# One chunk-causal attention and two MLPs on one core: a planner with other rules for results, ports and slots, and two score banks as one tile

## The chip, the cores and the metric

The kernel runs on one core of a Trainium2 chip. The metric is the device time of one execution in microseconds (us): the median of three runs of the kernel before is 953.37 us (953.12 to 954.3). Engines are named as the profile names them: PE (TensorE), DVE (VectorE), ACT (ScalarE), POOL (GpSimd), SP (SyncE, which issues the DMAs).

## The reference, cut to what matters

```python
def reference(q, k, v, moe, moe2):              # q, k, v: [4, 8, 576, 64] fp32
    scores = np.matmul(q, k.transpose(0, 1, 3, 2)) / np.sqrt(64)
    pos = np.arange(576)
    mask = pos[:, None] // 64 >= pos[None, :] // 64      # causal by chunks of 64
    scores = np.where(mask, scores, -1e9)
    scores -= scores.max(axis=-1, keepdims=True)
    a = np.exp(scores)
    a = a / (a.sum(axis=-1, keepdims=True) + 1e-9)
    x = np.matmul(a, v)                          # to [2304, 512]
    r = np.maximum(x @ moe.w_in, 0.0)            # 512 -> 2048
    x = (moe.s * (r * r) + moe.b) @ moe.w_out    # 2048 -> 512
    h = x @ moe2.w_in
    return np.maximum(0.01 * h, h) @ moe2.w_out
```

## The kernel before, in words

**The work.** The 576 positions are five blocks of queries, k = 0 to 4 (four of 128, one of 64), taken in the order 0, 1, 2, 4, 3; each block has 4 batches by 4 pairs of heads. For every block the kernel makes the attention, then runs the first MLP on the block's tokens in 16 chunks of the hidden width, while the attention of the next block is woven in between the chunks. fp32 operands are split into a high and a low part (`xh`/`xl`, `kh`/`kl`, `gh`/`gl`), and a product is three matmuls. L918 is the first matmul of that MLP ("h"), L934, L932 and L930 are its relu and its square, L936 and L937 the split of the result, L961 the second matmul ("y"). The second MLP comes last, with seven products in the place of eight: L1174 (banks "A", "B", "C") and L1239, copied out by L1149 (ACT) and added on by L1154 (DVE), with the leaky relu in L1188 and L1191.

**A head's attention.** The scores go into a PSUM bank `s` (L585 for k up to 1, L790 for k = 2 and 4, L830 for k = 3); then come a maximum, an exponential with its sum, the reciprocal of the sum, the norm (`p` times the reciprocal), the transposes on PE (L600), their copy to `pv` (L516 ACT, L518 DVE), and the product with v (L688, L869). For k = 2 and 4 a step handles two heads with two banks: two memsets of the masked corner (L796), two maxima (L797), two exponentials (L800), one add and one reciprocal for both (L805, L807), two norms (L809). For k = 3 the 576 scores of one head lie in two banks of 288: two maxima (L834) and a minimum of the two negated ones (L838), two exponentials (L841), add and reciprocal (L846, L848), one norm (L849). The norm of k = 1 is L577. Each norm may run on POOL or on DVE.

**What sets the order.** Nothing runs in the order of the source. Each operation is a `Step` with a cost per engine that may run it, the steps it comes after, the buffers that it opens and uses, and a due time. `Graph.order` plays this list forward: whenever an engine is idle it takes the ready step with the earliest due time, where a buffer is free. The order that comes out is issued as it stands on every engine. After a step's end the steps behind it become ready `LAT` = 0.04 later (0.18 for a step of POOL alone), for results of PE too. A step with `port=True` (the norms, splits and preparation of weights) starts only when no other such step runs on DVE or POOL:

```python
                    if s.port and e in ("DVE", "POOL") and port is not None or s.nbytes and out_there >= self.LANES:
                        continue
```

`after=` waits for the end of a step, `behind=` only for its issue. The products that add up in one bank (m_in, m_out, the second MLP's out_phase, the products with v) stand in an `after=` chain. `slot` cuts the buffer `pv` into slots, taken round robin. The pool of `s` has two tiles of one bank each; `bank("s", ...)` takes one of them, for scores and, in the second MLP, for the banks "B" and "C".

## Time and profile before

| what | us |
|---|---|
| median of three runs | 953.37 |
| the three runs | 953.12, 953.37, 954.3 |
| the profiled execution, its own time | 956.59 |
| span of that execution's trace | 954.8 |

All rows come from the one profiled execution. A row of the timeline gives the start, the duration, the engine, the line with its operation and, in brackets, how long the engine was idle before it and what ended that. PE overlaps its matmuls: a row of a matmul lasts longer than the time until the next can start. PEclk is the clock that PE was granted, as a share of 2.4 GHz.

### The profile page before, as it was taken

The page shows a single profiled execution, that of the slowest core. Times are in us where ns is not written, and L with a number is a line of the kernel's source. Part 1 is how long each engine was busy: PE and PEld are TensorE (multiplying, and loading weights), DVE is VectorE, ACT ScalarE, POOL GpSimd, SP SyncE. Part 2 cuts the span into 40 slices and gives each one's busy share as a digit, 9 for nine tenths or more (in the row PEclk, how much of TensorE's full clock was granted, in tenths as well). Part 3 has the DMA queues.
Part 4 walks back from the last instruction along what each step waited for, and adds up shares of the span by engine and source line. Part 5 has one row for each costly group of instructions (what it writes and reads, how often), then busy time and mean ns, then how long its engine had stood idle before and what let it go on. Part 6 is the DMA issues. An engine that isn't in the chain of part 4 may idle for free.

```text
span 954.8 us, 16614 instructions
## 1 busy us (share of the span) xinstructions
PE 935.8 (98%) x5780; PEld 828.2 (87%) x5780; DVE 659.0 (69%) x1321; ACT 564.7 (59%) x1198; POOL 103.5 (11%) x224
## 2 busy tenths in 40 slices
PE   9999999999999999999999999999999999999998
PEld 8677887777777888888878888899999999999998
DVE  5988878777587867766768664555595655855557
ACT  4766767675576656656558444454565646555443
POOL 1122221112121121122320000000000000000000
PEclk9999999999999999999999999999999999999999
DMA  8995487886748898587337981998229852147402
GB/s 235 341 303 184 130 290 222 287 308 181 231 136 262 262 303 260 153 251 233 110 94 236 383 284 60 372 417 363 98 61 330 309 183 100 50 181 292 162 1 67
DMA packets 147668, 208.27 MB, mean 218 GB/s; under 512 B 23552, under 2 KB 118400, under 8 KB 140928
## 3 DMA queue, kind: packets, MB, share of 16 engines
q1 hardware_dynamic: 145136, 206.42, 65.2%
q10 hardware_dynamic: 2448, 0.79, 0.4%
q8 instruction: 46, 0.75, 0.3%
q14 instruction: 38, 0.31, 0.1%
HBM read 154.47 MB, written 52.69 MB: 217 GB/s over the span
## 4 chain that ended last, share of the span: by engine, by line
PE 81%; DVE 6%; DMA 5%; ACT 2%; issue 2%; POOL 1%; SPq 1%; POOLq 0%; DVEq 0%; ACTq 0%
PE h L918 17%; PE y L961 16%; PE A L1239 10%; PE A L1174 10%; PE C L1174 5%; PE C L1239 5%; PE t L600 4%; PE o L869 4%; PE B L1239 3%; PE B L1174 2%; PE s L790 2%; PE s L585 1%; PE s L830 1%; PE warm L622 1%; DMA q<-in_q_dram 1%
## 5 line engine op out<-in xcount | busy, mean ns | idle before, releaser
L918 PE MATMUL h<-xh,w 128*128 128x512 f32 (+1 forms) x640 | 230.2, 389 | 2.2 <-DVE g L932 1.2
L961 PE MATMUL y<-gh,w 128*128 128x512 f32 (+1 forms) x640 | 185.8, 374 | 0.9 <-ACT yo L516 0.9
L918 PEld LDWEIGHTS h<-xh,w 128*128 128x128 f32 x640 | 119.2, 190 | 29.7 <-issue 4.1
L961 PEld LDWEIGHTS y<-gh,w 128*128 128x128 f32 x640 | 114.3, 188 | 21.2 <-ACT yo L516 1.2
L1232 ACT ACTIVATE gh<-G 128x384 fp32r<-128x384 f32 x168 | 86.9, 525 | 57.0 <-PE A L1239 21.6
L918 PE MATMUL h<-xl,w 128*128 128x512 f32 (+1 forms) x320 | 118.9, 372 | 0.7 <-DVE xl L698 0.7
L961 PE MATMUL y<-gl,w 128*128 128x512 f32 (+1 forms) x320 | 118.4, 370 | 0.0
L1174 PE MATMUL A<-xh,wi 128*128 128x384 f32 x384 | 112.9, 337 | 1.0 <-DVE G L1154 0.9
L1046 DVE TENSOR_TENSOR gl<-G,gh 128x384 fp32r<-128x384 f32 x168 | 91.4, 554 | 30.4 <-ACT gh L1232 28.7
L1239 PE MATMUL A<-gh,wo 128*128 128x384 f32 x384 | 98.0, 336 | 1.4 <-DVE Y L1154 1.4
L934 ACT ACTIVATE g<-h 128x512 f32<-128x512 f32 (+1 forms) x80 | 44.2, 553 | 84.1 <-PE h L918 77.2
L600 PE MATMUL t<-id_sb,p 128*128 128x128 f32 x400 | 67.5, 280 | 6.6 <-POOL p L577 3.1
L1174 PEld LDWEIGHTS A<-xh,wi 128*128 128x128 f32 x384 | 70.6, 188 | 2.9 <-DVE G L1154 1.5
L1239 PEld LDWEIGHTS A<-gh,wo 128*128 128x128 f32 x384 | 69.1, 188 | 2.4 <-DVE Y L1154 2.3
L961 PEld LDWEIGHTS y<-gl,w 128*128 128x128 f32 x320 | 60.3, 188 | 10.9 <-DVE gl L937 0.5
L600 PEld LDWEIGHTS t<-id_sb,p 128*128 128x128 f32 x400 | 46.8, 141 | 26.0 <-POOL p L577 5.9
L918 PEld LDWEIGHTS h<-xl,w 128*128 128x128 f32 x320 | 60.9, 190 | 8.2 <-DVE xl L698 1.0
L1188 ACT ACTIVATE G<-G 128x384 f32<-128x384 f32 x72 | 37.6, 524 | 47.2 <-DVE G L1154 47.2
L937 DVE TENSOR_TENSOR gl<-g,gh 128x512 fp32r<-128x512 f32 (+1 forms) x80 | 50.8, 635 | 20.1 <-ACT gh L936 16.5
L1174 PE MATMUL A<-xl,wi 128*128 128x384 f32 x192 | 64.5, 336 | 0.0
L1239 PE MATMUL A<-gl,wo 128*128 128x384 f32 x192 | 64.2, 335 | 0.0
L1046 DVE TENSOR_TENSOR G<-G 128x384 f32<-128x384 f32 x96 | 53.2, 555 | 12.8 <-ACT G L1188 11.2
(125 smaller groups left out, 1834.5 us busy)
## 6 DMA issues: line engine op xcount, KB each, us to landing
wi<-u_in SPq DMA_DIRECT2D x32, 896.0 KB, 7.8
wo<-u_out SPq DMA_DIRECT2D x28, 1024.0 KB, 9.0
w<-kept SPq DMA_DIRECT2D x16, 1024.0 KB, 7.9
u_in<-unit SPq DMA_DIRECT2D x16, 896.0 KB, 5.9
u_out<-unit SPq DMA_DIRECT2D x32, 448.0 KB, 4.6
early<-in_moe_w_in_dram SPq DMA_DIRECT2D x16, 512.0 KB, 5.9
early<-in_moe_w_out_dram SPq DMA_DIRECT2D x16, 512.0 KB, 6.4
kept<-w SPq DMA_DIRECT2D x8, 1024.0 KB, 7.7
```

Of the source, the lines that this page charges most:

```text
L600: e.transpose(tb()[:, x * 128:(x + 1) * 128], P()[:, pc:pc + 128], id_sb)
L790: e.matmul(out=o[h][:, :nk], lhsT=qs()[r, qc], rhs=kk()[r, :nk], start=(n == 0), stop=(n == 2))
L869: e.matmul(out=o()[64 * h:64 * h + 64, n * x:n * x + n], lhsT=V()[:, j, 64 * h:64 * h + 64], rhs=r, start=(j == 0), stop=(j == nj - 1),)
L918: e.matmul(out=h()[:, :T], lhsT=w()[:, wi, c * 128:(c + 1) * 128], rhs=x[blk, c]()[:, :T], start=(c == 0 and n == 0), stop=(c == KD - 1 an ...
L934: a = G.add({"ACT": act(T)}, lambda e: e.activation(out=g()[:, :T], in_=h()[:, :T], func=ACTF.Relu), [prev], [g], [h], due)
L937: lo = G.add({"DVE": dve(T)}, lambda e: e.tensor_tensor(out=gl()[:, :T], in0=g()[:, :T], in1=gh()[:, :T].bitcast(F32), op=ALU.subtract), [ ...
L961: e.matmul(out=y()[:, :W], lhsT=w()[:, wi, d * 128:(d + 1) * 128], rhs=x()[:, :W], start=(pos == 0 and n == 0), stop=(pos == NF - 1 and n ...
L1046: e.tensor_tensor(out=out, in0=x, in1=y, op=ALU.subtract)
L1174: e.matmul(out=x()[:, :NH], lhsT=in_w[n, i, c]()[:, s, ai], rhs=y()[:, c], start=(first and c == 0 and m == 0), stop=(c == 1 and m == 2), ...
L1188: {"ACT": act(NH)}, lambda e, y=y: e.activation(out=y(), in_=y(), func=ACTF.Lrelu), [a], [], [y], d2 + 2)
L1232: hi = G.add({"ACT": act(NH)}, lambda e, gh=gh, x=x: e.activation(out=gh(), in_=x(), func=ACTF.Copy), [a], [gh], [x], due - 2)
L1239: e.matmul(out=z[d]()[:, :NH], lhsT=out_w[n, r]()[:, 2 * i + d, s], rhs=y(), start=(first and i == 0 and m == 0), stop=(i == 3 and m == 2) ...
```

## The change

**The planner.** A result of PE is taken to be there `DRAIN` later than the matmul ends (0.14, 0.25 or 0.32 by the kind of matmul). A port step no longer excludes another: POOL may start beside a DVE step, and its step is taken to go on at 0.4 of its speed as long as DVE holds the port (`HELD`). Slots of `pv` are taken by which one came free first. Products into one bank are chained with `behind=`. Loads of v for the second block wait no longer for the first block's attention.

**The scores.** The two banks `s` become one tile `[128, 2, 512]`. For k = 2 and 4 one memset and one maximum cover both heads. For k = 3 one maximum and one exponential cover both halves, and the minimum goes. Lines move: L577 to L614, L600 to L637, L790 to L830, L796/L797 to L834/L835, L805/L807 to L843/L845, L809 to L847, L830 to L870, L849 to L882, L869 to L902, L918 to L952, L961 to L995, L1154 to L1188, L1174 to L1208.

The core of the diff:

```diff
     LANES = 8
+    DRAIN = {"f": 0.14, "r": 0.25, "c": 0.32}
+    HELD = 0.6
...
                 elif what == "room":
-                    room[s] += 1
+                    room[s.key] += 1
+                    slots[s.key].append(s.slot)
                 elif what == "free":
                     idle[e] = True
-                    if port is s:
-                        port = None
+                elif what == "pool":
+                    if e == turn_no:
+                        idle["POOL"], busy = True, None
...
-                    if s.port and e in ("DVE", "POOL") and port is not None or s.nbytes and out_there >= self.LANES:
+                    if s.nbytes and out_there >= self.LANES:
                         continue
...
+                if e in ("DVE", "POOL") and s.port:
+                    if e == "POOL":
+                        busy = [s, s.eng[e] - self.AGAIN[e], t]
+                    elif busy is not None:
+                        u = min(max(held, busy[2]), t)
+                        busy[1:] = busy[1] - (1 - self.HELD) * (u - busy[2]) - (t - u), t
+                    if e == "DVE":
+                        held = end
+                    if busy is not None:
+                        w = max(held - t, 0.0)
+                        left = busy[1]
+                        left = left / (1 - self.HELD) if left <= w * (1 - self.HELD) else left + w * self.HELD
...
+                if e == "PE":
+                    end += self.DRAIN[s.mode]
                 heapq.heappush(events, (end, n, "done", s, e))
...
-        "h": (ps("ps_h", 1), 1), "s": (ps("ps_s", 2), 2), "t": (ps("ps_t", 1), 1),
+        "h": (ps("ps_h", 1), 1), "s": (ps("ps_s", 1), 2), "t": (ps("ps_t", 1), 1),
...
-            i = taken[name, k] = taken.get((name, k), -1) + 1
-            x = i % npt * ptn if name == "pt" else npt * ptn + i % nv * vn
+            x = b.slot * ptn if name == "pt" else npt * ptn + b.slot * vn
...
+            s_t.append(pools["s"][0].tile([128, 2, 512], F32, tag="s", name="s"))
+        return s_t[0]
...
+            b = Buf("s", lambda: s_both()[:, b.slot])
...
-            vl = [G.add({"SP": 0.65}, v_load, before, fresh, [V4], due=due - 8, run=512, nbytes=512 * (nk // 128 * 128))]
+            vl = [G.add({"SP": 0.65}, v_load, before if blk > 1 else [], fresh, [V4], due=due - 8, run=512, nbytes=512 * (nk // 128 * 128))]
...
-                for h in range(2):
-                    mk = G.add({"DVE": 0.13}, lambda e, x=bk[h]: e.memset(x()[:64, nk - 64:nk], NEG), [sc], uses=[bk[h]], due=due - 4.5)
-                    mx.append(G.add({"DVE": dve(nk)}, lambda e, nm=nm, h=h, x=bk[h]: e.reduce_max(out=nm()[:, h:h + 1], in_=x()[:, :nk], axis=AX.X, negate=True),
-                                    [mk], [nm] * (h == 0), [nm, bk[h]], due=due - 4))
+                mk = G.add({"DVE": dve(128)}, lambda e: e.memset(s_both()[:64, :, nk - 64:nk], NEG), [sc], uses=bk, due=due - 4.5)
+                mx = [G.add({"DVE": dve(2 * nk)}, lambda e, nm=nm: e.reduce_max(out=nm()[:, 0:2], in_=s_both()[:, :, :nk], axis=AX.X, negate=True),
+                            [mk], [nm], [nm, *bk], due=due - 4)]
...
+                mx = G.add({"DVE": dve(nk)}, lambda e, nm=nm: e.reduce_max(out=nm()[:, 0:1], in_=s_both()[:, :, :half], axis=AX.XY, negate=True),
+                           [sc], [nm], [nm, *bk], due=due - 4)
+                ex = G.add({"ACT": act(nk, 1, True)}, lambda e, nm=nm, l=l, P=P: e.activation(
+                    out=P()[:, :nk].rearrange("p (j n) -> p j n", j=2), in_=s_both()[:, :, :half], func=ACTF.Exp, bias=nm()[:, 0:1], scale=1.0,
+                    accum_out=l()[:, 0:1]), [mx], [l], [P, l, nm, *bk], due - 3.5)
...
-                {"PE": 3 * (T / 2400 + 0.013)}, fn, [prev, w_ok[blk, f, 0], *x_ok[blk, c]], [h] * (c == 0),
-                [h, w, xh_t[blk, c], xl_t[blk, c]], due + c * 0.01,
+                {"PE": 3 * (T / 2400 + 0.013)}, fn, [w_ok[blk, f, 0], *x_ok[blk, c]], [h] * (c == 0),
+                [h, w, xh_t[blk, c], xl_t[blk, c]], due + c * 0.01, behind=[prev] * (c > 0),
```

**Order on DVE, in the block k = 2.** `s` are the scores, `nm` the negated maxima, `l` the sums, `unit` a piece of the second MLP's weights. Before:

```order
L796 MEMSET s 64x64 x2
L713 SCALAR_TENSOR_TENSOR qs<-q,qs 128x128
L797 TENSOR_REDUCE nm<-s 128x1 x2
L716 TENSOR_TENSOR kl<-k,kh 128x384
L464 SCALAR_TENSOR_TENSOR unit<-unit 128x1024
L805 TENSOR_SCALAR l<-l 128x2
L807 RECIPROCAL l<-l 128x2
```

The change:

```order
L834 MEMSET s 64x2x64
L555 COPY pv<-t 128x256
L835 TENSOR_REDUCE nm<-s 128x2
L751 SCALAR_TENSOR_TENSOR qs<-q,qs 128x128
L754 TENSOR_TENSOR kl<-k,kh 128x384
L515 TENSOR_TENSOR unit<-unit 128x2x128 x3
L843 TENSOR_SCALAR l<-l 128x2
L515 TENSOR_TENSOR unit<-unit 128x2x128
L845 RECIPROCAL l<-l 128x2
L847 TENSOR_SCALAR p<-p,l 128x384
```

Memset and maximum come once for two heads, and one of the two norms of the pair (L847) stands on DVE, behind the reciprocal; the other stands on POOL. In the whole order 42 norms move from POOL to DVE: 11 of 32 for k = 1, 16 of 32 for k = 2 and 15 of 31 for k = 4, where one had been on DVE.

**Order on PE where the attention of k = 3 begins.** `t` are transposes, `o` the products with v. Before:

```order
L830 MATMUL s<-kh,qs 128x288
L830 MATMUL s<-kl,qs 128x288
L830 MATMUL s<-kh,qs 128x288
L600 MATMUL t<-id_sb,p 128x128 x2
L918 MATMUL h<-xh,w 128x512
L918 MATMUL h<-xl,w 128x512
L918 MATMUL h<-xh,w 128x512
L830 MATMUL s<-kh,qs 128x288
L830 MATMUL s<-kl,qs 128x288
L830 MATMUL s<-kh,qs 128x288
L869 MATMUL o<-pv 64x128 x24
```

The change, where the transposes of the first head of k = 3 end the piece:

```order
L870 MATMUL s<-kh,qs 128x288 x2
L870 MATMUL s<-kl,qs 128x288
L870 MATMUL s<-kh,qs 128x288
L952 MATMUL h<-xh,w 128x512
L952 MATMUL h<-xl,w 128x512
L952 MATMUL h<-xh,w 128x512
L870 MATMUL s<-kh,qs 128x288
L870 MATMUL s<-kl,qs 128x288
L870 MATMUL s<-kh,qs 128x288 x2
L870 MATMUL s<-kl,qs 128x288
L870 MATMUL s<-kh,qs 128x288
L637 MATMUL t<-id_sb,p 128x128 x4
```

The scores of a head come in one piece of six. Between the first head's last score (the row ahead of `h`) and its transposes there stand three matmuls of the MLP and the scores of the next head.

**Order on PE in the second MLP.** The number behind a name tells tiles apart. Before, where B comes directly ahead of C:

```order
L1174 MATMUL B_8239<-xh2_7950,wi_7163 128x384
L1174 MATMUL B_8239<-xl2_7985,wi_7163 128x384
L1174 MATMUL B_8239<-xh2_7950,wi_7163 128x384
L1174 MATMUL B_8239<-xh2_7950,wi_7192 128x384
L1174 MATMUL B_8239<-xl2_7985,wi_7192 128x384
L1174 MATMUL B_8239<-xh2_7950,wi_7192 128x384
L1174 MATMUL C_8249<-xh2_7885,wi_7215 128x384
L1174 MATMUL C_8249<-xl2_7888,wi_7215 128x384
L1174 MATMUL C_8249<-xh2_7885,wi_7215 128x384
L1174 MATMUL C_8249<-xh2_7885,wi_7249 128x384
L1174 MATMUL C_8249<-xl2_7888,wi_7249 128x384
L1174 MATMUL C_8249<-xh2_7885,wi_7249 128x384
```

The change, the units C, B, C of one pass:

```order
L1208 MATMUL s_288<-xh2_7690,wi_8019 128x384
L1208 MATMUL s_288<-xl2_7725,wi_8019 128x384
L1208 MATMUL s_288<-xh2_7690,wi_8019 128x384
L1208 MATMUL s_288<-xh2_7690,wi_8031 128x384
L1208 MATMUL s_288<-xl2_7725,wi_8031 128x384
L1208 MATMUL s_288<-xh2_7690,wi_8031 128x384
L1208 MATMUL s_288<-xh2_7649,wi_8019 128x384
L1208 MATMUL s_288<-xl2_7661,wi_8019 128x384
L1208 MATMUL s_288<-xh2_7649,wi_8019 128x384
L1208 MATMUL s_288<-xh2_7649,wi_8031 128x384
L1208 MATMUL s_288<-xl2_7661,wi_8031 128x384
L1208 MATMUL s_288<-xh2_7649,wi_8031 128x384
```

B and C had a tile each; now both are the one tile `s_288`. The first and the third unit add up in one bank, the second goes to the other. In the program as built, a reader of one bank waits for the last write into either, and a write into one for the readers of both: in the second MLP 31 units of PE wait for a DVE add (L1188) that reads the other bank. In two places, as at the third unit here, the unit waits for ACT's copy (L1183) of its own bank, and that copy waits for the unit just ahead; in three more there is one unit of other work between.

## Rows read from the trace of the kernel before

**Rows 1.** Page, busy time of each engine, share of the span, instructions.

```profile
PE 935.8 (98%) x5780; PEld 828.2 (87%) x5780; DVE 659.0 (69%) x1321; ACT 564.7 (59%) x1198; POOL 103.5 (11%) x224
```

**Rows 2.** Waits of TensorE: line, releaser: us in all, times, longest us.

```profile
PE t L600 <- POOL p L577: 3.1, 3, 1.6
PE t L600 <- POOL p L809: 2.6, 4, 1.7
PE A L1239 <- DVE Y L1154: 1.4, 3, 0.5
PE warm L622 <- POOL wq L512: 1.3, 1, 1.3
PE h L918 <- DVE g L932: 1.2, 2, 1.1
PE y L961 <- ACT yo L516: 0.9, 1, 0.9
...
PE A L1174 <- DVE G L1154: 0.9, 2, 0.7
...
PE t L600 <- ACT pv L516: 0.2, 1, 0.2
```

**Rows 3.** Timeline, 236 to 240 us: start, us, engine line op, [idle before <-releaser].

```profile
236.02 2.91 POOL L809 TENSOR_SCALAR p<-p,l 128x384 f32<-128x384 f32 x2 [5.18 <-DVE l L807]
...
236.26 2.22 DVE L485 TENSOR_TENSOR unit<-unit 128x1792 f32<-128x1792 f32 x1 [0.43 <-ACT unit L484]
...
237.03 0.27 PE L600 MATMUL t<-id_sb,p 128*128 128x128 f32 x1
...
238.99 0.55 PE L600 MATMUL t<-id_sb,p 128*128 128x128 f32 x3 [1.68 <-POOL p L809]
```

**Rows 4.** Busy times from 240.0 to 243.5 us; behind the engines stands PEclk.

```profile
240.00:243.50 3.50, 3.50 (x13) 2.70 (x10) 3.17 (x8) 2.79 (x9) 0.00 (x0) 0.54 0.96 284
```

**Rows 5.** Timeline, 491.9 to 494 us.

```profile
491.92 0.41 PE L961 MATMUL y<-gh,w 128*128 128x258 f32 x2
...
492.12 0.39 ACT L934 ACTIVATE g<-h 128x256 f32<-128x256 f32 x1 [0.53 <-PE h L918]
...
492.86 0.69 POOL L809 TENSOR_SCALAR p<-p,l 128x512 f32<-128x512 f32 x1 [3.29 <-DVE l L807]
...
492.90 0.93 DVE L809 TENSOR_SCALAR p<-p,l 128x512 f32<-128x512 f32 x1
```

**Rows 6.** Groups by form: shapes xcount | busy us, mean ns | idle before.

```profile
L809 POOL TENSOR_SCALAR p<-p,l 128x512 f32<-128x512 f32 x31 | 21.5, 701 | 74.1 <-DVE l L807 55.5 <-PE y L961 11.2 <-ACT gh L936 7.5
...
L345 DVE TENSOR_SCALAR early<-early 128x512 int32<-128x512 int32 x2 | 0.8, 420 | 0.0
```

**Rows 7.** Groups by form, parts of the softmax and of its operands.

```profile
L834 DVE TENSOR_REDUCE nm<-s 128x1 f32<-128x288 f32 x32 | 13.8, 450 | 1.1 <-PE s L830 1.0
...
L716 DVE TENSOR_TENSOR kl<-k,kh 128x576 fp32r<-128x576 f32 x16 | 12.0, 750 | 0.3
...
L715 ACT ACTIVATE kh<-k 128x576 fp32r<-128x576 f32 x16 | 10.8, 674 | 0.0
...
L841 ACT ACTIVATION_READ_ACCUMULATOR p<-s,nm 128x1 f32 x32 | 6.4, 200 | 0.0
...
L838 DVE TENSOR_SCALAR nm<-nm 128x1 f32<-128x1 f32 x16 | 3.3, 205 | 0.0
```

**Rows 8.** Timeline, 609 to 612 us, in the second MLP.

```profile
609.04 0.47 ACT L1149 ACTIVATE G<-A 128x384 f32<-128x384 f32 x1
...
609.86 0.56 DVE L1154 TENSOR_TENSOR G<-C,G 128x384 f32<-128x384 f32 x1 [1.29 <-ACT G L1149]
...
610.37 0.34 PE L1174 MATMUL A<-xl,wi 128*128 128x384 f32 x1
...
610.54 0.33 PE L1174 MATMUL A<-xh,wi 128*128 128x384 f32 x1
...
611.53 0.45 PE L1174 MATMUL A<-xh,wi 128*128 128x384 f32 x1 [0.65 <-DVE G L1154]
```

More of the change, by code (lines that the diff above doesn't have):

```diff
@@ L92, in order @@
         room = dict(self.room)
+        slots = {k: list(range(n)) for k, n in room.items()}
         idle = {e: True for s in self.steps for e in s.eng}
@@ L95, in order @@
         events, n, out_there = [], 0, 0
-        port, dma, mode = None, 0.0, "f"
+        dma, mode, busy, held, turn_no = 0.0, "f", None, 0.0, 0
         out = []
@@ L167, in order @@
                 s.at, s.on, idle[e] = t, e, False
-                if s.port and e in ("DVE", "POOL"):
-                    port = s
                 out.append(s)
@@ L587, in scores @@
             fresh.add(bk)
-            out.append(G.add({"PE": max(n * 1.67e-3, 0.214) - 0.06}, fn, after, new, [bk, *q, *kk], due - 5))
+            out.append(G.add({"PE": max(n * 1.67e-3, 0.214) - 0.06}, fn, after, new, [bk, *q, *kk], due - 5, behind=out[-1:]))
         return out
@@ L825, in later_block, with fn @@
                 kh, kl_, qs, ok = score_parts(Q, K, nk, ql, kl, due)
-                sc = []
-                for j in range(2):
-                    def fn(e, j=j, bk=bk, kh=kh, kl=kl_, qs=qs):
+                def fn(e, bk=bk, kh=kh, kl=kl_, qs=qs):
+                    for x in bk:
+                        x()
+                    for j in range(2):
                         for n, (qc, kk) in enumerate(((0, kh), (0, kl), (1, kh))):
-                            e.matmul(out=bk[j]()[:, :half], lhsT=qs()[:, qc], rhs=kk()[:, half * j:half * j + half], start=(n == 0), stop=(n == 2))
-                    sc.append(G.add({"PE": 3 * (half / 2400 + 0.013)}, fn, ok, [bk[j]], [kh, kl_, qs], due - 5))
+                            e.matmul(out=s_both()[:, j, :half], lhsT=qs()[:, qc, :128], rhs=kk()[:, half * j:half * j + half], start=(n == 0), stop=(n == 2))
@@ L832, in later_block @@
+                sc = G.add({"PE": 6 * (half / 2400 + 0.013)}, fn, ok, bk, [qs, kh, kl_], due - 5)
                 nm, l = buf("sm", [128, 8], F32, "nm"), buf("sm", [128, 8], F32, "l")
-                mx = [
-                    G.add({"DVE": dve(half)}, lambda e, j=j, bk=bk, nm=nm: e.reduce_max(out=nm()[:, j:j + 1], in_=bk[j]()[:, :half], axis=AX.X, negate=True),
-                          [sc[j]], [nm] * (j == 0), [nm, bk[j]], due - 4)
-                    for j in range(2)
-                ]
@@ L838, in later_block @@
-                neg = G.add({"DVE": 0.2}, lambda e, nm=nm: e.tensor_scalar(
-                    out=nm()[:, 0:1], in0=nm()[:, 0:1], scalar1=nm()[:, 1:2], scalar2=None, op0=ALU.min), mx, uses=[nm], due=due - 4)
-                ex = [
-                    G.add({"ACT": act(half, 1, True)}, lambda e, j=j, bk=bk, nm=nm, l=l, P=P: e.activation(
-                        out=P()[:, half * j:half * j + half], in_=bk[j]()[:, :half], func=ACTF.Exp, bias=nm()[:, 0:1], scale=1.0,
-                        accum_out=l()[:, j:j + 1]), [neg], [l] * (j == 0), [P, l, nm, bk[j]], due - 3.5)
-                    for j in range(2)
-                ]
@@ L848, in later_block @@
+                a = G.add({"DVE": 0.17}, lambda e, l=l: e.tensor_scalar(
+                    out=l()[:, 0:1], in0=l()[:, 0:1], scalar1=1e-9, scalar2=None, op0=ALU.add), [ex], uses=[l], due=due - 3)
                 a = G.add({"DVE": 0.16}, lambda e, l=l: e.reciprocal(out=l()[:, 0:1], in_=l()[:, 0:1]), [a], uses=[l], due=due - 3)
@@ L877, in later_block @@
             xf = xf_t[k, p]
-            a = G.add({"PE": many * nj * 0.206 * n / 128}, av, [x for c in pair for x in c[3]], [o] + [xf] * (pair[0][0] == 0), [xf, *[x for c in pair for x in (c[2], c[4])]], due, mode="c")
+            a = G.add({"PE": many * nj * 0.206 * n / 128}, av, [x for c in pair for x in c[3]], [o] + [xf] * (pair[0][0] == 0), [xf, *[x for c in pair for x in (c[2], c[4])]], due, mode="c", behind=[last_av])
+            last_av = a
             b0 = pair[0][0]
@@ L1242, in out_phase @@
                 after = [hi, lo, out_ok[n, r], *[ev.get(({6: 1, 7: 6, 4: 7, 3: 5}.get(r), d)) for d in range(2)]]
-                p = G.add({"PE": ONE}, fn, after, z if first and i == 0 else [], [*z, gh, gl, out_w[n, r]], due)
+                p = G.add({"PE": ONE}, fn, after, z if first and i == 0 else [], [*z, gh, gl, out_w[n, r]], due, behind=[p] if i else [])
             for d in range(2):
```

45 lines of the change are left out of this document (30 added, 15 removed).

## The prediction

> **What bounds the kernel now.** I read the page's busy times first. PE is busy for 935.8 us of a span of 954.8, DVE for 69% and ACT for 59% of it [rows 1]: PE is the bound, and all that any order of the same matmuls can win lies in PE's 19.0 idle us and in what its clock costs. The order of the change holds the same matmuls, so I price waits alone.
>
> The waits of PE come next [rows 2]. The largest are the transposes that wait for a norm on POOL (3.1 and 2.6 us), the second MLP's units that wait for a DVE add (1.4 and 0.9), the start-up (`warm`, 1.3) and, in the first MLP, "h" behind a square on DVE (1.2). The view has 14 lines, which sum to 14.4 us in 23 waits; the first and the last stand in the group with the largest of the rest, and one that is left out (0.2, the norm of k = 3) belongs to the softmax. A row of PE outlasts the moment at which the next could start: matmuls of 384 columns start 0.17 apart and have rows of 0.34 [rows 8]. So a wait costs about 0.17 more than its idle time, 23 x 0.17 = 3.9 in all.
>
> The timeline shows how the longest wait arises [rows 3]. Two norms of a pair stand one behind the other on POOL, beside a DVE step of 2.22 us with two inputs; together they last 2.91 where two of them elsewhere last 1.4 [rows 6], and PE's second transpose comes 1.68 us late. Right behind it PE was granted 0.54 of its clock, its lower level of 1.2 GHz nearly throughout 3.5 us [rows 4]; at the upper level that work would have taken 1.7 us less. The view of stretches has no other such dip before the end.
>
> So PE loses 14.4 + 3.9 + 1.7 = **20.0 us**: norms 5.9 + 8 x 0.17 = 7.3; second MLP 2.3 + 5 x 0.17 = 3.1; the first MLP, the evacuations and the start 6.2 + 10 x 0.17 = 7.9; the clock 1.7. The profiled execution took 956.59 us, 0.3% over the median of 953.37; I take the loss to be the same in both and subtract from the median. About 0.2%, 1.9 us, is what a measurement of this kernel can tell from no change.
>
> **The change, part by part.**
>
> *Lag of PE's results.* The planner counted 0.04 us from the end of a matmul to its reader. In the trace the relu starts 0.20 after the MLP's next matmul could take PE [rows 5]: 492.12 against 491.92. With 0.14 more the planner counts 0.18, about what the row shows, and places more PE work between a unit and what needs its result. This is to take most of the small waits of the first MLP and the evacuations. Of 7.9 I leave the start (1.5 with its share, its steps don't change) and 2.0 for queues on ACT and DVE. Bounds: 0 and 6.4 remaining.
>
> *Norms on two engines.* 42 norms go to DVE. A pair then lasts from 492.86 to 493.83, 0.97, where POOL alone takes two times 0.70 [rows 5, 6]: 0.4 us come off the chain of a head pair. Against that, DVE is held for 0.93, and a norm of this width without POOL beside it is nearest to a DVE step of 0.42 on 512 [rows 5, 6]: 42 x 0.51 = 21 us more DVE time. DVE is 69% busy, so most of that is idle time of DVE used up; I charge PE **2.0** of it, a tenth, with ends at 0 and 21. The norm waits of 7.3 shrink to **1.0**, since a pair no longer queues on POOL and PE has mostly 4 to 8 us of work behind a head's scores against a chain of about 4.
>
> *One maximum, one exponential.* For k = 3, two maxima of 0.45 and a minimum of 0.2 become one maximum over 576, which I take at 0.75, as a DVE step on 576 elements, and two exponentials with 0.2 each for their sums become one of 0.67 + 0.2 [rows 7]. For the flat blocks 32 memsets and 32 maxima go. These are hidden behind PE already and priced at nothing, except through the head chains: were the cover gone, each would count once per head.
>
> *Where k = 3 begins.* The order on PE has three "h" matmuls and six scores between the first head's scores and its transposes. By columns from 0.17 for 384 [rows 8] that is 3 x 0.23 + 6 x 0.13 = 1.5 us. The chain is 0.20 lag + 0.75 + 0.67 + 0.20 + two small steps of 0.20 + a norm of at least 0.70 [rows 5 to 7] + hand-overs, about 3.2. **1.7 us** of waiting arise here that the order before did not have. Bounds: 1.0, if the chain hands over faster than I add up, and 3.4, if the norm meets a DVE step as in [rows 3] or the wait costs clock.
>
> *Products chained by issue, slots by first free, loads of v.* They only let the planner place steps earlier. PE runs in order, so nothing on the chip waits less for it; priced at nothing, and included in the order whose waits I count. No DMA is added or taken away, and no wait of PE in [rows 2] is for a load.
>
> *One tile for two banks.* This adds waits. A copy or add of bank B or C now waits for the last matmul into either bank, and a unit into one for the readers of both. In the second MLP two units must wait for a copy that can begin only when the unit just ahead has ended: 0.20 + 0.47 + 0.05 = 0.72 each [rows 5, 8]. Three have one unit of work (6 x 0.17 = 1.04) against lag, copy, add and hand-overs, 0.20 + 0.47 + 0.56 + 0.15 = 1.4, so 0.35 each. Together 2.5; with 1.0 for queues on ACT and DVE (before, the 3.1 were mostly such queueing: 0.65 late at 611.53 behind an add that ACT's copy had delayed [rows 8]) the second MLP loses **3.4**, 0.3 more than before. At the start, two steps wait for an evacuation of the other bank, one evacuation of 0.47 each [rows 8]: **0.9**.
>
> *Clock.* A dip followed the longest wait [rows 3, 4]; without that wait I count none.
>
> Sum after: start 1.5 + first MLP 2.0 + DVE held 2.0 + norms 1.0 + k = 3 1.7 + second MLP 3.4 + tile at the start 0.9 = **12.5**. 20.0 - 12.5 = 7.5 less: 953.4 - 7.5 = **945.9 us**.
>
> The Trainium skill (SBUF — State Buffer, section on who interferes with whom) says that DVE and GpSimd share one port pair as an exclusive lock, held for a whole instruction, the other blocking fully. By it the norm on DVE would end 0.42 after POOL's, 493.97; the row has 493.83, so the trace agrees only in part. By that rule the DVE half of a pair takes 1.07 in place of 0.93, and 42 of them 6 us more DVE time.
>
> **The rivals.**
>
> *The tile ties the second MLP (slower).* 31 units of PE wait there for an add on the other bank. They mostly have 2.1 us or more of other work against a chain of 1.4: a margin of about 0.65. If the queues of ACT and DVE make the chain 1.0 longer, two steps of 0.5 ahead in the queue, each unit comes 0.35 late: 31 x 0.35 = 10.9, less the 1.0 already counted, gives 955.8. It decides against the change from about 0.33 us of mean lateness beyond the margin. For it: with separate banks an add already came 0.65 late [rows 8]. Against it: that was one of only five such waits [rows 2], and the planner places these steps with the lag in view.
>
> *DVE held beside POOL (no change).* If each moved norm delays PE by 0.2 through the splits and copies queued behind it on DVE, 42 x 0.2 = 8.4 come back in place of 2.0: 952.3. For it: DVE is held 0.51 longer per norm [rows 5, 6] and "pv" copies and splits stand behind it. Against it: the norm replaces one that PE waited for in rows of 3.1 and 2.6.
>
> *The planner gets all that it can (faster still).* Only the waits written into the order stay: start 1.5, k = 3 1.7, second MLP 2.5, tile at the start 0.9, in all 6.6: 953.4 - 13.4 = 940.0. For it: the small waits have one cause, the lag of 0.20 where 0.04 was planned. Against it: queueing on engines that are 60 to 70% busy does not vanish.
>
> **How the numbers follow.** Forecast 0.63, the tile 0.10, DVE held 0.12, the planner's best 0.15. The forecast's own bounds (first MLP 0 to 6.4 remaining, k = 3 1.0 to 3.4, a new dip of 1.7) are about 942 to 952. Range 938.5 to 954: it takes in the planner's best and DVE held, and leaves out the tile and the far ends, less than 2 in 10. Faster by over 0.2% is below 951.5: 0.60 of the forecast, 0.15, and 0.03 of DVE held, 0.78. Same (to 955.3): 0.12. Slower: 0.10.
>
> **What would show it.** In the changed profile the transposes' waits for the norm should fall from 5.9 us to under 2 outside the start of k = 3, where a wait of 1 to 2 us for the norm (L882) should stand. L847 and L614 should have some 40 rows on DVE, near 0.9 when POOL runs beside. The second MLP should show two waits of about 0.7 of L1208, on ACT's copy, and its sum of waits should stay near 3. PEclk should have no dip before the end. The prediction is wrong if the second MLP's waits grow past 8 us (the tile), if PE's waits move to DVE's copies and splits (DVE held), or if the waits of "h" and "y" for ACT and DVE stay as they are, which would say that the lag was not their cause.

## The result and the profile after

The change made the kernel slower: 961.03 us median (960.32 to 962.35) against 953.3 of the kernel before on the same chip, a ratio of 1.0081 with a 95% interval of 1.0066 to 1.0096. The forecast was 945.9, the range 938.5 to 954. The profiled execution of the change has a span of 959.3 us.

The page's row of busy times, which answers to [rows 1]:

```profile
PE 935.1 (97%) x5780; PEld 827.6 (86%) x5780; DVE 677.5 (71%) x1277; ACT 556.6 (58%) x1156; POOL 92.4 (10%) x182
```

PE is busy for the same 935 us; the span is 4.5 us longer, and PE's idle time has grown from 19.0 to 24.2 us. DVE has 18.5 us more, ACT 8 less. The waits of PE, which answer to [rows 2] (the ten largest of 18 lines; all 18 sum to 19.6 us, before to 14.4):

```profile
PE t L637 <- ACT pv L553: 2.5, 2, 2.1
PE t L637 <- POOL p L614: 2.4, 4, 1.2
PE h L952 <- DVE l L879: 2.1, 1, 2.1
PE t L637 <- DVE p L607: 2.0, 1, 2.0
PE A L1208 <- DVE G L1188: 1.5, 2, 0.7
PE A L1273 <- DVE Y L1188: 1.4, 3, 0.5
PE warm L659 <- POOL wq L549: 1.3, 1, 1.3
PE s L952 <- DVE xl L935: 1.2, 1, 1.2
PE s L1208 <- ACT G L1183: 1.2, 2, 0.6
PE t L637 <- POOL p L847: 1.1, 1, 1.1
```

The transposes' waits for norms on POOL have shrunk from 5.9 to 3.5 us. But there are new ones, three of them of 2 us each: for the split `xl` where k = 3 begins (named "DVE l L879" here; the split is the DVE step just ahead of that one, as a timeline below shows), for the norm of block 0 at the start (L607), and for a copy of transposes (L553). (By k = 3 this document means the block with 576 scores a head, by k = 4 the one with 512; in the kernel's own count they are blocks 4 and 3.) In the second MLP, units of L1208 wait for adds (L1188) and copies (L1183), 1.5 and 1.2 us, where adds had taken 0.9. And the clock fell twice, where the profiled execution before has one fall [rows 4]:

```profile
32.00:36.00 4.00, 3.31 (x12) 2.82 (x13) 3.29 (x6) 2.16 (x3) 0.00 (x0) 0.57 1.06 315
292.00:296.00 4.00, 4.00 (x15) 3.28 (x14) 3.44 (x8) 2.38 (x6) 0.71 (x5) 0.58 1.09 309
```

Behind the engines stands PEclk, 0.57 and 0.58 of 2.4 GHz, so about 1.7 us were lost in each stretch of 4 us. The list of runs gives each run's mean granted clock: 0.995 to 0.998 in the change's four, and 0.999 or 1.000 in 70 of 73 runs of the kernel before, over the comparisons of the experiments below. The other three have 0.998 and took 956.2 to 957.3 us. The profiled execution of before (956.59 us, 0.998) was like these three.

### The profile page after: what moved, and what is told of

It is laid out like the page before. It is cut to its first block, busy times and chain, and to the rows that moved or that the text cites. A ratio compares the mean times of both kernels' runs of the same rounds, so it can differ in the third digit from the quotient of the medians.

```text
span 959.3 us, 16512 instructions
## 1 busy us (share of the span) xinstructions
PE 935.1 (97%) x5780; PEld 827.6 (86%) x5780; DVE 677.5 (71%) x1277; ACT 556.6 (58%) x1156; POOL 92.4 (10%) x182
## 4 chain that ended last, share of the span: by engine, by line
PE 83%; DVE 7%; ACT 4%; issue 2%; DMA 2%; POOL 1%; SPq 0%; DVEq 0%; ACTq 0%; POOLq 0%
PE y L995 18%; PE h L952 14%; PE A L1273 10%; PE A L1208 9%; PE s L1208 8%; PE C L1273 5%; PE o L902 4%; PE t L637 4%; PE s L952 3%; PE s L1273 3%; PE s L830 2%; PE s L622 2%; PE s L870 1%; PE warm L659 1%; DMA k<-in_k_dram 1%
## 5 line engine op out<-in xcount | busy, mean ns | idle before, releaser
L995 PE MATMUL y<-gh,w 128*128 128x512 f32 (+1 forms) x640 | 187.7, 377 | 0.7 <-ACT yo L553 0.7
L952 PE MATMUL h<-xh,w 128*128 128x512 f32 (+1 forms) x552 | 184.9, 387 | 1.1 <-ACT xh L933 0.8
L995 PEld LDWEIGHTS y<-gh,w 128*128 128x128 f32 x640 | 113.2, 188 | 21.5 <-issue 2.6
L952 PEld LDWEIGHTS h<-xh,w 128*128 128x128 f32 x552 | 102.5, 190 | 24.2 <-issue 3.0
L995 PE MATMUL y<-gl,w 128*128 128x512 f32 (+1 forms) x320 | 118.3, 370 | 0.0
L1208 PE MATMUL A<-xh,wi 128*128 128x384 f32 x384 | 111.9, 336 | 1.7 <-DVE G L1188 1.5
L952 PE MATMUL h<-xl,w 128*128 128x512 f32 (+1 forms) x276 | 102.1, 370 | 2.3 <-DVE l L879 2.1
L1208 PE MATMUL s<-xh,wi 128*128 128x384 f32 x288 | 84.5, 338 | 1.7 <-ACT G L1183 1.2
L1188 DVE TENSOR_TENSOR G<-s,G 128x384 f32<-128x384 f32 x48 | 26.5, 556 | 72.4 <-PE s L1208 64.2
L1208 PEld LDWEIGHTS A<-xh,wi 128*128 128x128 f32 x384 | 70.6, 188 | 2.7 <-DVE G L1188 2.1
L637 PE MATMUL t<-id_sb,p 128*128 128x128 f32 x384 | 63.9, 279 | 8.4 <-ACT pv L553 2.5
L995 PEld LDWEIGHTS y<-gl,w 128*128 128x128 f32 x320 | 60.3, 188 | 10.8 <-DVE gl L971 0.5
L637 PEld LDWEIGHTS t<-id_sb,p 128*128 128x128 f32 x384 | 45.8, 142 | 25.1 <-issue 5.5
L1208 PE MATMUL A<-xl,wi 128*128 128x384 f32 x192 | 64.4, 335 | 0.0
L971 DVE TENSOR_TENSOR gl<-g,gh 128x512 fp32r<-128x512 f32 (+1 forms) x80 | 51.7, 646 | 16.0 <-ACT gh L970 15.9
L968 ACT ACTIVATE g<-h 128x512 f32<-128x512 f32 (+1 forms) x69 | 38.0, 550 | 42.1 <-PE h L952 39.4
```

What stands on the lines that cost most here:

```text
L637: e.transpose(tb()[:, x * 128:(x + 1) * 128], P()[:, pc:pc + 128], id_sb)
L952: e.matmul(out=h()[:, :T], lhsT=w()[:, wi, c * 128:(c + 1) * 128], rhs=x[blk, c]()[:, :T], start=(c == 0 and n == 0), stop=(c == KD - 1 an ...
L968: a = G.add({"ACT": act(T)}, lambda e: e.activation(out=g()[:, :T], in_=h()[:, :T], func=ACTF.Relu), [prev], [g], [h], due)
L971: lo = G.add({"DVE": dve(T)}, lambda e: e.tensor_tensor(out=gl()[:, :T], in0=g()[:, :T], in1=gh()[:, :T].bitcast(F32), op=ALU.subtract), [ ...
L995: e.matmul(out=y()[:, :W], lhsT=w()[:, wi, d * 128:(d + 1) * 128], rhs=x()[:, :W], start=(pos == 0 and n == 0), stop=(pos == NF - 1 and n ...
L1188: e.tensor_tensor(out=out, in0=in_, in1=out, op=ALU.add)
```

## The experiments

Theory A: the one tile costs the time. Theory B: the new order does, by a few long waits and the clock behind them. All times are medians, with the ratio to the kernel before in the same comparison; before stood at 953.5 to 954.0 in all of them.

### The halves of the change

**planner_only.** The planner in full, but the score tiles and softmax steps of before:

```diff
-        "h": (ps("ps_h", 1), 1), "s": (ps("ps_s", 1), 2), "t": (ps("ps_t", 1), 1),
+        "h": (ps("ps_h", 1), 1), "s": (ps("ps_s", 2), 2), "t": (ps("ps_t", 1), 1),
...
-                sc = G.add({"PE": 6 * (half / 2400 + 0.013)}, fn, ok, bk, [qs, kh, kl_], due - 5)
+                    sc.append(G.add({"PE": 3 * (half / 2400 + 0.013)}, fn, ok, [bk[j]], [kh, kl_, qs], due - 5))
```

> Edit: the change's planner in full, but two separate score tiles of one bank and the memsets, maxima, minimum and exponentials as before. Theory A (the one tile costs the time: waits of PE for the other bank, in the second MLP and at the start, 4 to 5 us): between 949 and 954, the second MLP's waits of PE back to 3 us from 6.7. Theory B (the planner's new order costs it: long waits at 32, 290, 449 and 505 us with two clock dips): slower than before, 956 to 959, with waits of PE of 1 to 2.5 us in the first MLP again, though perhaps at other places.

957.47 us, 1.004 (1.0027 to 1.0052): slower, as B had it. The second MLP's waits are not back at 3 us, but the reason is one place at its entry:

```profile
595.23 1.72 SPq L529 DMA_DIRECT2D u_out<-unit  x2
...
  ACT gh L1269: 4.0, 1
...
601.24 0.52 ACT L1269 ACTIVATE gh<-G 128x384 fp32r<-128x384 f32 x1 [3.98 <-issue]
...
602.20 0.44 PE L1211 MATMUL A<-xh,wi 128*128 128x384 f32 x1 [2.95 <-ACT G L1186]
```

ACT stands idle for 3.98 us ahead of a split (L1269) which waits for the stores of prepared weights (`u_out<-unit`): the second row is from the view of L529, under "who waited for it". In the built program the split's buffer takes the place of theirs. Behind it on ACT is the copy that PE waits for, 2.95 us. The clock fell there too (0.86 and 0.72 from 600 to 608 us).

**tile_only.** The kernel before, with the one tile and the merged steps (and the bookkeeping that tells which bank of the tile is free):

```diff
-        "h": (ps("ps_h", 1), 1), "s": (ps("ps_s", 2), 2), "t": (ps("ps_t", 1), 1),
+        "h": (ps("ps_h", 1), 1), "s": (ps("ps_s", 1), 2), "t": (ps("ps_t", 1), 1),
...
+        if key == "s":
+            b = Buf("s", lambda: s_both()[:, b.slot])
```

> Edit: the planner of before in full (lag 0.04, one port, after= chains, slots round robin), but the one score tile with one memset and one maximum, and one exponential for k = 3. Theory A (the tile costs the time): 957 to 961, and the second MLP's PE waits at 5 us or more, since the planner here does not even count a lag. Theory B (the planner): 951 to 955, since one maximum shortens DVE's work by some 10 us and the tie costs little with this order.

960.24 us, 1.0074 (1.0061 to 1.0088): slower, as A had it, but not where A had it. The second MLP's waits are small; new ones stand at the start, where block 0 keeps transposes and products in `s`:

```profile
PE s L702 <- ACT pv L530: 0.7, 1, 0.7
PE s L599 <- ACT xh L710: 0.7, 1, 0.7
...
PE s L614 <- DVE xl L712: 0.5, 1, 0.5
```

These waits do not explain the loss. All of `tile_only`'s waits sum to 15.6 us, 1.2 more than before, and its granted clock is 1.000; PE is busy for 938.4 us where it had been for 935.8. Most of the 6.5 us stays unexplained. So both halves cost time, but only of the first are the places found. The sum of the two (3.8 + 6.5 us) is more than the change's 7.7.

**drain0.** The change without the lag:

```diff
-    DRAIN = {"f": 0.14, "r": 0.25, "c": 0.32}
+    DRAIN = {"f": 0.0, "r": 0.0, "c": 0.0}
```

> Edit: the change with a lag of 0 for PE's results in place of 0.14, 0.25 and 0.32. If the lag is what keeps small waits away, as the prediction had it, they come back: 3 to 6 us slower than the change, 964 to 967. If the change's loss is in a few long waits that any new order may or may not have, this is another order and comes out anywhere from 953 to 962, with its long waits at other places and the count of small waits little different.

975.5 us, 1.0234 (1.022 to 1.0248): slower than either expectation. The transposes wait 6.8 us for norms of L614, in seven waits, and one unit of the second MLP 3.7 us for an add. Beside the other new rules, the plan without the lag is 14.5 us worse; that is one order, and which of the rules needs the lag was not run.

**lag_only.** The kernel before with the lag and nothing else:

```diff
+    DRAIN = {"f": 0.14, "r": 0.25, "c": 0.32}
...
+                if e == "PE":
+                    end += self.DRAIN[s.mode]
```

> Edit: the kernel before with the lag of PE's results alone (0.14, 0.25, 0.32), and nothing else of the change; products into one bank stay chained by the end of the one before. If the lag by itself takes the small waits away, as the prediction's first term had it: 945 to 951. If it works only together with chains by issue, since the planner otherwise counts a lag between two products that PE issues without one, the order is spread needlessly: 957 to 965, with PE's waits at new places.

961.07 us, 1.0078 (1.0063 to 1.0093): the second expectation. PE waits five times for the square (2.2 us together), and the place at the entry of the second MLP is there again (3.8 us). The lag alone is no gain. It also brings the wait of 1.98 us for block 0's norm at the start (at 32.2 us): `planner_only` and the change have it, and the kernel before, `tile_only` and `drain0`, the orders without the lag, do not.

### Two edits that leave the order alone

**l2_split.** The order on every engine is that of the change; only B and C of the second MLP lie in two tiles:

```diff
-        A, B, C = bank("h" if i % 2 == 0 else "t", "A"), bank("s", "B"), bank("s", "C")
+        A, B, C = bank("h" if i % 2 == 0 else "t", "A"), bank("s2", "B"), bank("s2", "C")
```

> Edit: the changed kernel with the same order on every engine, but in the second MLP the banks B and C are two tiles of one bank; attention and first MLP as in the change. Theory A: the four waits for ACT's copy and the add behind it (0.75 and 0.91, twice) and the four of 0.29 go, 4.5 us, so 956.5. Theory B in its pure form (the second MLP's waits are of the order, not of the tile): the same waits stay, for the banks themselves, 960 to 961.5. No effect elsewhere: PE's waits before 595 us as in the change.

954.5 us (950.78 to 957.33, 11 runs), 1.001 (0.9996 to 1.0024). So the tie in the second MLP cost 6.5 us, by medians that are good to a microsecond or two; the profiled executions, both at a clock of 0.996, differ by 5.6 (959.3 and 953.7). No wait of a unit of the first product (L1208, here L1214) for an add or copy is left in the list of waits. The timeline of the change shows how the tie works, at one of two places alike:

```profile
778.21 0.34 PE L1208 MATMUL s<-xh,wi 128*128 128x384 f32 x1
778.59 0.49 ACT L1183 ACTIVATE G<-s 128x384 f32<-128x384 f32 x1 [1.59 <-PE s L1208]
...
779.13 0.44 PE L1208 MATMUL s<-xh,wi 128*128 128x384 f32 x1 [0.58 <-ACT G L1183]
...
780.48 1.02 DVE L1188 TENSOR_TENSOR G<-s,G 128x384 f32<-128x384 f32 x2 [6.10 <-PE s L1208]
...
782.66 0.55 DVE L1188 TENSOR_TENSOR G<-A,G 128x384 f32<-128x384 f32 x1
...
783.26 0.44 PE L1208 MATMUL A<-xh,wi 128*128 128x384 f32 x1 [0.74 <-DVE G L1188]
```

C's six matmuls end near 777.5 and B's are the last ones, up to 778.55, and ACT's copy of C starts at 778.59: it waited for B. The third unit waits for that copy, 0.58 us idle; it starts at 779.13, 0.75 after the time at which the next matmul could start (778.21 + 0.17). Then DVE adds B and C together at 780.48, both late. On ACT and DVE the leaky relu, a split and at last, at 782.66, the add of A stand behind them, and PE waits for that one as well, 0.74. With two tiles the copy starts right behind C's own unit, while PE writes B:

```profile
776.78 0.49 ACT L1189 ACTIVATE G<-C 128x384 f32<-128x384 f32 x1 [0.55 <-PE C L1214]
```

**fill32.** Six more warming matmuls, in the idle stretch ahead of the wait for L607:

```diff
-    FILL = 26
+    FILL = 32
```

> Edit: the change with six more warming matmuls (32 in place of 26), all of them in the place at the start where PE stands idle for 2 us before the transposes of p; nothing else moves on any engine. If the half clock from about 33 to 36 us follows from that idle stretch, it goes, and with it some 1.6 us: 959.4. If the clock falls for another reason (the long stretch of work before it, or power), the time stays at 960.5 to 961.5 and the dip stays.

958.62 us (957.23 to 961.98), 1.0057 (1.0044 to 1.007). 2.4 us come back, and in the profiled execution the clock holds at the start:

```profile
32.00:36.00 4.00, 4.00 (x26) 3.12 (x26) 4.00 (x7) 2.76 (x4) 0.00 (x0) 1.00 0.89 298
```

The stretch had 0.57 in the change. Idle time of 2 us led to the fall here; it does not always. `split_stay6` below has the same idle stretch and 1.00 in its profile. And the change's own wait of 2.06 us at 449 us was followed by 1.00 (448 to 452 us), where the same wait in `fill32` was followed by 0.75 and 0.83 (448 to 456 us).

**split_fill.** The two edits together (`bank("s2", ...)` and `FILL = 32`):

> Edit: both clean edits together, two tiles in the second MLP and the six warming matmuls. If they are independent, their effects add: 954.5 of the split alone less 1.6, 952.9. The other dip, behind the wait where k = 3 begins, stays.

953.3 us, 1.0001 (0.9991 to 1.001). Beside the split the six matmuls take 1.2 us off, where 1.6 was expected and they had taken 2.4 alone; the interval of the split's run is 1.3 us either way, so whether the two effects add in full is not shown.

### Other orders

The wait where k = 3 begins, in the change:

```profile
285.40 1.70 ACT L521 ACTIVATE unit<-unit 128x1792 fp32r<-128x1792 f32 x1 [2.19 <-DVE unit L515]
...
286.60 0.29 PE L870 MATMUL s<-kh,qs 128*128 128x288 f32 x1
...
287.01 0.61 ACT L933 ACTIVATE xh<-xf 128x512 fp32r<-128x512 f32 x1
...
287.60 2.02 DVE L522 TENSOR_TENSOR unit<-unit 128x1792 f32<-128x1792 f32 x1
...
287.67 0.51 PE L952 MATMUL h<-xh,w 128*128 128x512 f32 x1 [0.78 <-ACT xh L933]
...
289.53 0.68 DVE L935 TENSOR_TENSOR xl<-xf,xh 128x512 fp32r<-128x512 f32 x1
290.13 0.14 DVE L879 TENSOR_SCALAR l<-l 128x1 f32<-128x1 f32 x1
...
290.27 0.50 PE L952 MATMUL h<-xl,w 128*128 128x512 f32 x1 [2.10 <-DVE l L879]
```

On ACT `xh` stands behind a weight step of 1.70 us (L521). DVE starts another of 2.02 us (L522) at 287.60, 0.02 us before `xh` is there (287.01 + 0.61). The split `xl`, which the next "h" needs, starts behind it at 289.53, and PE stands for 0.78 and 2.10 us. The due time of `xl` in the planner is far earlier than that of the weight step, but a step that is ready takes an idle engine.

**split_stay6.** Two tiles, and another order from the end of k = 2. `STAY` is what the planner charges PE, in its ranking, for a turn from one kind of matmul to another:

```diff
-    STAY = 10.0
+    STAY = 6.0
```

> Edit: two tiles in the second MLP, and the planner's price for a turn of PE's mode 6 in place of 10, which leaves the order as it is up to the last heads of k = 2 and gives another one from there: the 2-us preparation of weights on DVE no longer stands ahead of the split that the first h of the next block needs. If that place costs what the trace shows (waits of 0.9 and 2.4 us and half clock for 3.5 us), the time is 3 to 4 us under the 954.5 of the split: 951, with one dip (at the start) left. If long waits come up elsewhere in any new order, 953 to 956.

948.61 us, 0.9947 (0.9936 to 0.9959): 5.9 us under the split alone, more than expected. The clock was 1.000 in three of five runs. The waits of 0.78 and 2.10 us have shrunk to 0.4 and 0.3, and others of the old order are gone: for the copy L553 near 449 us and for the norm of k = 2 at 279 us.

**split_fill_stay4.** Two tiles, `FILL = 32`, `STAY = 4.0`:

> Edit: two tiles in the second MLP, the six warming matmuls, and 4 as the price of a turn: an order without a wait of PE over 1.5 us in the plan. If the three named losses (the tile in the second MLP, the long waits, the clock behind them) are the whole loss of the change, this is 947 to 950, faster than the kernel before by 0.4 to 0.7%, with no dip of the clock before the end. If the remaining ties of the one tile in attention or queueing cost as much again, 951 to 954.

**946.47 us, 0.9933 (0.9921 to 0.9946): faster than both kernels**, 14.6 us under the change. The kernel before was not run with `FILL = 32` or `STAY = 4.0`, so how much of this belongs to the change is not shown. No stretch of 4 us before the end has a PEclk under 0.97. Its largest waits of PE:

```profile
PE t L642 <- POOL p L619: 2.2, 4, 1.2
PE A L1279 <- DVE Y L1194: 1.4, 3, 0.5
PE warm L664 <- POOL wq L554: 1.3, 1, 1.3
PE s L957 <- DVE xl L940: 1.2, 1, 1.2
PE o L907 <- DVE pv L560: 0.8, 1, 0.8
```

**best_h05.** The same with `HELD = 0.5`:

> Edit: the fastest kernel so far with 0.5 in place of 0.6 for how far a DVE port step holds POOL: another order, with fewer holes in the plan. If what counts is the holes that the planner leaves and not the value itself, 943 to 947; if the value counts (POOL is held more, not less, in the trace: norms of 1.04 and 0.92 us on POOL), late norms return and it is 947 to 951.

947.08 us, 0.9933 (0.9916 to 0.995). It lies where the two expectations meet. The transposes' waits for POOL rise from 2.2 to 4.3 us, and other waits go: the value hardly counts for the time.

### What the parts are worth with the harm gone

**best_port.** The fastest kernel with the old port rule, so that all norms run on POOL:

```diff
-                    if s.nbytes and out_there >= self.LANES:
+                    if s.port and e in ("DVE", "POOL") and port is not None or s.nbytes and out_there >= self.LANES:
```

> Edit: the fastest kernel so far (two tiles in the second MLP, six warming matmuls, 4 for a turn) with the old port rule of the planner: every norm goes back to POOL. If norms on DVE take the waits of the transposes away (7.3 us by the prediction), 950 to 954, with the transposes' waits for POOL back at 5 us or more. If they are worth little because POOL beside DVE is what is slow and two norms on POOL fit behind PE's work anyway, 945 to 949.

954.76 us, 1.0005 (0.9996 to 1.0015). But the transposes do not wait more for POOL:

```profile
PE A L1218 <- ACT G L1193: 3.4, 2, 2.4
PE t L646 <- POOL p L623: 2.5, 3, 1.2
```

What is lost is again the entry of the second MLP. **po_fill_stay4**, with two score tiles and the softmax steps of before, loses at that place too:

> Edit: the planner of the change with two separate score tiles and the softmax steps of before (no merged maximum), the six warming matmuls and 4 as the price of a turn. If the merged maximum and exponential are worth something once the tile's ties in the second MLP are gone, this is slower than the 946.5 of the like kernel with the merged steps: 949 to 953. If they are worth nothing, 945 to 948.

955.41 us, 1.0017 (1.0008 to 1.0027). Neither can be read for what its edit is worth, so the four last runs hold the first splits back in the plan, and ACT's copy goes ahead:

```diff
-                hi = G.add({"ACT": act(NH)}, lambda e, gh=gh, x=x: e.activation(out=gh(), in_=x(), func=ACTF.Copy), [a], [gh], [x], due - 2)
+                hi = G.add({"ACT": act(NH)}, lambda e, gh=gh, x=x: e.activation(out=gh(), in_=x(), func=ACTF.Copy), [a], [gh], [x], due - 2, rel=begin[NB] + 17 if n == 0 else 0.0)
```

> Edit: the fastest kernel (946.5) with the same hold, where the split already stood behind that copy. A control: no loss stood at that place, so no gain, 945.5 to 948.

The control: 947.04 us, 0.9929 (0.9918 to 0.9941), no change.

> Edit: every norm on POOL by the old port rule (954.8), with the same place cured. If norms on DVE are worth something by themselves, this stays at 951 or more against 946.5; if what was lost was the place at the entry of the second MLP, 947 to 950. The waits of transposes for norms on POOL stay at 2 to 3 us either way, as they were at 2.8.

949.91 us, 0.9963 (0.995 to 0.9976): the second expectation, at its upper end. What is left for norms on DVE is 2.9 us, and the transposes' waits for norms are 2.8 us as before.

> Edit: separate score tiles and the softmax steps of before, six warming matmuls, 4 for a turn (955.4), with the same place cured. What is then left between it and the like kernel with the merged steps (946.5) is what merged maximum and exponential are worth with the second MLP's banks apart: if nothing, 946 to 949; if they shorten the heads' chains as the prediction's chain has it, 950 to 952.

951.61 us, 0.9975 (0.9964 to 0.9986): against the control, merged maximum and exponential are worth 4.6 us. Both numbers are between two orders that differ in many places, so they hold to a microsecond or two at best. The lists of waits differ by 1.1 us only (10.4 and 9.3), so where the 4.6 come from is not shown.

> Edit: the planner alone (separate score tiles, old softmax steps), and the first split of the second MLP is held back in the plan by 17 us, so that ACT's next copy stands ahead of it; it had waited 4 us for a store of prepared weights, with PE behind it. If that one place and the clock behind it are what made the planner alone slower than before (957.5), it falls by 4 to 6 us to 951.5 to 953.5, no change against the kernel before. If not, it stays at 956 to 958.

953.2 us, 0.9991 (0.9979 to 1.0003): the planner alone is no slower than before once that place is cured, as the first expectation had it, and no faster. It still has the wait at the start (2.27 us) and a clock of 0.997 or 0.998 in all 12 runs. `po_rel` is the same planner with `FILL = 32` and `STAY = 4.0`, and it is 0.25% faster than before.

## Why the prediction was wrong

The step that failed is the sum after, 12.5 us. Counted in the prediction's own way (idle time in the list of waits, 0.17 for each wait, the clock), the change loses 19.6 + 26 x 0.17 + 3.4 = 27.4 us:

| term | forecast | measured |
|---|---|---|
| start, with the tile there | 1.5 + 0.9 | 4.9 |
| first MLP and evacuations | 2.0 | 5.9 |
| DVE held | 2.0 | in the other rows |
| norms on POOL | 1.0 | 4.4 |
| where k = 3 begins | 1.7 | 3.2 |
| second MLP | 3.4 | 5.7 |
| clock | 0 | 3.4 |

By this count the change is 7.4 us slower, and it was 7.7. That is close in part by luck: the base of 20.0 was too large, and the list leaves out four waits of 0.13 us in the second MLP.

**The base.** "I take the loss to be the same in both" failed. The fall of the clock (1.7 us; by [rows 4] 3.5 x 0.46 = 1.6) that was booked as a gain belonged to the one profiled execution; the timed runs of before hold 0.999 to 1.000. Some 3 us of the 20.0 were not there to be won.

**The second MLP: 3.4 us, "0.3 more than before".** The two units at 0.72 came out at 0.75. Missed was what the late copy pushes: B's and C's adds come late on DVE, and A's add, behind them and a split, costs PE 0.91 from start to start at the same two places; four more units lose 0.29 each. That is 2 x 0.75 + 2 x 0.91 + 4 x 0.29 = 4.5 us. The second matmul behind each of the eight waits starts another 0.11 late, in all 5.4, and with two tiles, where all of this is gone, the kernel is 6.5 us faster. The term looked at whom PE waits for, and not at what else waits in the queue of that engine.

**Where k = 3 begins: 1.7 us.** The place was right, the mechanism was not. The norm of the first head was hidden; PE waited for `xh` and `xl`, behind long weight steps on ACT and DVE, 0.78 + 2.10 us, after 1.09 for a norm of k = 2 held up by DVE. Another order from there on, with the clock behind these waits, is worth 5.9 us; it changes later places too.

**The clock: "I count none".** Two falls, 3.4 us, behind the idle stretches of 1.98 us at the start and 2.10 us at k = 3. The start was taken as unchanged (1.5); its order on PE is new, and the stretch there comes with the lag, as `lag_only` shows.

**The lag.** "This is to take most of the small waits": of the first MLP and the evacuations 4.9 us of idle time stayed, 2.5 of it for copies of transposes (L553) and 1.2 for `xl` at 505 us. By itself the lag makes the sum of all waits larger, 17.6 us against 14.4 (`lag_only`). The planner as a whole is worth nothing measurable in one order (`planner_rel`) and, with the warming matmuls and the other price of a turn, 0.25% (`po_rel`); the change without the lag is far worse (`drain0`).

**Norms on DVE.** The waits for norms on POOL fell, but not for this reason: with all norms on POOL they are 2.5 and 0.3 us (`port_rel`), against 2.2 and 0.2 in the fastest kernel. The price was wrong as well. From one row of 0.93 DVE was to be held; the groups by form show that POOL mostly is:

```profile
L847 POOL TENSOR_SCALAR p<-p,l 128x384 f32<-128x384 f32 x16 | 16.6, 1035 | 95.9 <-DVE l L845 83.1 <-ACT g L968 12.8
...
L847 POOL TENSOR_SCALAR p<-p,l 128x512 f32<-128x512 f32 x16 | 14.6, 915 | 79.3 <-DVE l L845 57.5 <-ACT g L964 7.0 <-PE h L952 5.5
...
L847 DVE TENSOR_SCALAR p<-p,l 128x512 f32<-128x512 f32 x16 | 9.1, 567 | 1.4
...
L847 DVE TENSOR_SCALAR p<-p,l 128x384 f32<-128x384 f32 x16 | 6.7, 418 | 1.3
```

DVE's norms last 0.42 and 0.57 us, and POOL's grow from means of 0.70 for either width to 1.04 and 0.92. But the 0.57 is a mean of two cases, and which engine pays goes by which one starts first. Of the 16 pairs of 512 columns, DVE starts first in 13, as at 426 us, and POOL in three, as at 503.87:

```profile
426.36 0.49 DVE L847 TENSOR_SCALAR p<-p,l 128x512 f32<-128x512 f32 x1
426.44 0.96 POOL L847 TENSOR_SCALAR p<-p,l 128x512 f32<-128x512 f32 x1 [3.34 <-ACT g L964]
...
503.87 0.75 POOL L847 TENSOR_SCALAR p<-p,l 128x512 f32<-128x512 f32 x1 [5.26 <-ACT xh L933]
...
503.98 0.92 DVE L847 TENSOR_SCALAR p<-p,l 128x512 f32<-128x512 f32 x1
...
504.82 0.67 DVE L935 TENSOR_TENSOR xl<-xf,xh 128x512 fp32r<-128x512 f32 x1
...
505.55 0.50 PE L952 MATMUL s<-xl,w 128*128 128x512 f32 x1 [1.17 <-DVE xl L935]
```

Where DVE is first its norm lasts 0.49 and POOL's, in 12 of the 13, 0.96 or more; in the 13th DVE's is nearly done when POOL's starts. In the three others POOL's lasts 0.70 to 0.75 and DVE's 0.91 or 0.92. The row of 0.93 was a pair with POOL first, by 0.04 us [rows 5]; the new order puts DVE first in most.

The Trainium skill (SBUF — State Buffer, the section on who interferes with whom) has it that whichever of the two starts first keeps the shared port for its whole instruction, and the other blocks. The trace agrees on who pays, not on all of the price: at 426 us full blocking would end POOL's norm at 426.85 + 0.70 = 427.55, and it ends at 427.40.

The timeline at 276 us shows what a stream of DVE steps does to POOL:

```profile
276.29 0.68 DVE L971 TENSOR_TENSOR gl<-g,gh 128x512 fp32r<-128x512 f32 x1
...
276.55 2.86 POOL L847 TENSOR_SCALAR p<-p,l 128x384 f32<-128x384 f32 x1 [4.69 <-DVE l L845]
...
276.88 0.42 DVE L847 TENSOR_SCALAR p<-p,l 128x384 f32<-128x384 f32 x1
...
277.21 0.69 DVE L935 TENSOR_TENSOR xl<-xf,xh 128x512 fp32r<-128x512 f32 x1
...
277.81 1.23 DVE L501 SCALAR_TENSOR_TENSOR unit<-unit 128x1024 int32<-128x1024 int32 x1
```

The norm on POOL starts at 276.55 beside L971. Three more DVE steps follow, each starting before the one ahead has ended, and POOL's norm ends at 279.41, 0.37 us behind the last of them. POOL is passed over at each change from one DVE step to the next.

**The merged steps: "priced at nothing".** With two tiles in the second MLP and the new planner they are worth some 4.6 us, the largest of the parts that were measured by themselves. With the old planner and the tie they were no gain (`tile_only`).

**The rivals.** The tile's rival had the sign and the engine, at a chance of 0.10 and with 955.8 us. Its mechanism, 31 units each a little late by queueing, is not what the trace shows: eight units were late, by the tie and what it pushes, and none of them with two tiles (`l2_split`). DVE held occurred at one place: at 505 us PE waits 1.17 us for the split `xl`, which stands on DVE behind a norm held for 0.92 (the rows above), and with all norms on POOL that wait is 0.27 (`port_rel`). The sum of the planner's best (940.0) was not reached by any order tried.

What stays open: why the clock fell behind 2 us of idle time in some places and executions and not in others; most of what `tile_only` lost; and the one wait of 2.1 us for L553 near 449 us, which no run isolated. There the copy stands on ACT behind the step L753, which had waited 1.24 us, by the trace for the merged maximum on DVE (L835, 1.23 us). `best_port` has a like wait of 1.75 us at 431 us.

## What to carry to other kernels

Two banks in one tile were one thing to the program that waits on them: share a tile where one instruction reads both, and give every other use of those banks tiles of their own. A list scheduler's change is a new order everywhere, and what it was worth here was decided in large part by three or four places where a long step, a store or a block's border meets the engine that bounds the kernel; find those places in the new order, with what stands ahead in each queue, before the average gain is summed. And take the base for a sum from an execution that is like the timed ones: the run list's clock told here that the profiled one was not.

## What the runs showed of the hardware that was not expected

Of a pair of norms of 512 columns side by side, the engine that starts second pays: GpSimd's took 0.96 us in place of 0.70 where VectorE's had started 0.06 to 0.09 us ahead, and VectorE's 0.92 in place of 0.49 where GpSimd's was ahead by 0.05 to 0.11. One GpSimd step beside VectorE steps that follow each other without a gap was let in only behind the last of them, and lasted 2.86 us. Of the change's three waits of PE of about 2 us, two were each followed by a stretch of 4 us with 0.57 or 0.58 of the clock, which nearly doubled their price, and the third was not; six warming matmuls took one of these falls away. One maximum over 1,024 score columns takes 1.22 us where two over 512 took 2 x 0.68.
